# A new prologue for a spectral filter followed by a mixer: filter loads on another queue, deeper weight loading, a shorter float64 rounding and a new order

## The chip, the cores and the metric

The kernel runs on one core of one Trainium2 chip. In this kernel TensorE does the matrix products (10624 matmuls), whose results go to tiles in the memory PSUM; VectorE and ScalarE work element by element; Pool (GpSimd) and SyncE mainly issue transfers (DMA; 244 of Pool's 249 counted instructions). A "granted clock" is the profile's figure for the speed that TensorE was allowed, as a share of full speed. The metric is the device time of one execution, in microseconds (us). The kernel before took 3224.24 us (median of 3 runs, 3223.76 to 3224.53).

## The reference

The input `x` has 8 batches of 3008 positions by 256 channels. First a filter in the frequency domain, then an MLP mixer over positions and over channels. The four mixer weights are float64.

```python
X = np.fft.rfft(x, axis=1)
y = np.fft.irfft(X * (filt_r + 1j * filt_i)[None], n=3008, axis=1).astype(np.float32)
h  = np.maximum(y.transpose(0, 2, 1) @ w_tok1, 0.0) @ w_tok2      # (3008,256), (256,3008)
u  = y + h.transpose(0, 2, 1)
h2 = np.maximum(u @ w_ch1, 0.0) @ w_ch2                            # (256,1536), (1536,256)
return (u + h2).astype(np.float32)
```

## The kernel before

The transform of 3008 = 64 * 47 points is done in two steps. A batch passes through twelve length-64 transforms (a matmul, a copy by ScalarE, a store to the DRAM scratch `z`), then 32 length-47 transforms with the filter product in between (a matmul, six VectorE operations, a matmul, a copy, a store to the scratch `g`). The mixer reads `g` back into tiles called t4; its first work on a batch is a length-64 inverse transform, which VectorE copies out of PSUM as `y`.

Before the first batch can be mixed, 40 blocks of float64 weights must be rounded to float32 on the chip: 12 blocks of w1 (`w_tok1`), 16 of w2 (`w_tok2`, 376 columns each), 6 of wc1 and 6 of wc2 (512 columns each). A block lands in a staging tile as pairs of 32-bit words.

```python
    xp = pool("xp", 4)
    t4p = pool("t4p", NXC + 2)          # NXC = 12
    up = pool("up", 2)
    ...
    def filt_load():
        nc.vector.memset(filt, 0.0)
        for src, p0 in ((filt_r, 0), (filt_i, HALF)):
            nc.scalar.dma_start(filt[p0:p0 + A]..., raw(src, 0, [[64 * D, A], [1, K2 * D]]))
            lo = p0 + 32
            nc.scalar.dma_start(filt[lo:lo + A - 1, 1:K2, :],          # the mirrored rows, line 179 (L179)
                                raw(src, 63, [[64 * D, A - 1], [-D, K2 - 1], [1, D]]))
            nc.scalar.dma_start(filt[lo:lo + A, 0, :], raw(src, 32, [[64 * D, A], [1, D]]))

    def stage(n):
        return up.tile([P, n], I64, tag="u", name="st")

    def rounded(st, n, parts):          # lo, hi: the lower and upper words of the block
        ...
        nc.vector.tensor_scalar(out=top_i, in0=hi, scalar1=0x7FFFFFFF, scalar2=None, op0=ALU.bitwise_and)
        nc.vector.tensor_scalar(out=top, in0=top, scalar1=HI_MAX, scalar2=2.0 ** -112, op0=ALU.min, op1=ALU.mult)
        nc.vector.tensor_scalar(out=rest_i, in0=top_i, scalar1=3, scalar2=0x7F800000,
                                op0=ALU.logical_shift_left, op1=ALU.bitwise_and)
        nc.vector.tensor_scalar(out=top_i, in0=top_i, scalar1=3, scalar2=None, op0=ALU.logical_shift_left)
        nc.vector.scalar_tensor_tensor(out=rest, in0=lo, scalar=2.0 ** -52, in1=rest, op0=ALU.mult, op1=ALU.mult)
        nc.vector.tensor_tensor(out=top, in0=top, in1=rest, op=ALU.add)
        for src, dst in parts:          # the sign: reads hi once more
            nc.vector.scalar_tensor_tensor(out=dst.bitcast(U32), in0=src(hi), scalar=0x80000000, in1=src(top_i),
                                           op0=ALU.bitwise_and, op1=ALU.bitwise_or)
    ...
        filt_load()
        convert = weights()             # each step loads one block and rounds the one before
        for _ in dft(GROUPS[0]):        # batch 0: one block beside each step of the transforms
            next(convert, None)
        for _ in convert:
            pass
        for c in range(NXC):
            t4_load(0, c)
        ...                             # the steady phase: mixer of a batch, filter of later batches beside it
```

Of the kernel before, what the change touches and what calls it, by code (L numbers as in the profile page):

```python
# [16 lines left out]
# The sequence of 3008 = 64 * 47 positions is n = 47 * n2 + n1, with n1 = 24 * h + a.  # L17
# [7 lines left out]
K2 = 32          # residues of the frequency mod 64, up to its sign  # L25
A = 24           # n1 in two halves of 24; (h, a) = (1, 23) is padding
KR = 4 * A       # rows (h, re/im, a) of one residue
HALF = 64
HI_MAX = float(np.array(0x47EFFFFF, np.uint32).view(np.float32))    # float32's largest, as a float64's upper word
XC = 2           # columns a in one chunk of the length-64 transforms  # L30
NXC = A // XC
KC = 2           # residues in one load or store of the length-47 transforms
WC = 2           # residues in one load of their matrices
# [5 lines left out]
MT = 6           # tiles of 512 positions: four columns a, each (h, n2)  # L39
NG = 8           # n2 in one load of the second token weights  # L40
GROUPS = ((0,), (1, 2), (3, 4), (5, 6), (7,))    # batches whose filter runs together


def _make_tables():
    """The real transform of 3008 points in two steps, and its inverse.

    wa: over n2, to (h, re/im, k2) from (h, n2). The residues 0 and 32 are real and share one slot.
    wb: over n1, twiddles included, to (re/im, q), for each k2. q < 24 is the frequency k2 + 64 q, and
        q = 32 + j - 1 is 64 j - k2 (64 j - 32 for k2 = 0).
    wi, wai: the inverses of wb and wa, with the 1/N in wi; the imaginary parts of the first and  # L50
        last frequency don't count.
    """
# [3 lines left out]
    for h in range(2):  # L56
        r = slice(h * 64, h * 64 + 64)
        for k2 in range(K2):
            th = 2 * np.pi * ((n2 * k2) % N2) / N2
            c, s = np.cos(th), np.sin(th)  # L60
            re, im = h * 64 + k2, h * 64 + 32 + k2
# [47 lines left out]
def kernel(  # L109
# [20 lines left out]
    # Between the two steps the rows change partitions, by way of DRAM.  # L130
# [7 lines left out]
    xp = pool("xp", 4)  # L138
# [6 lines left out]
    t4p = pool("t4p", NXC + 2)  # L145
# [10 lines left out]

    wa = glob.tile([P, P], FP32, name="wa")
    wai = glob.tile([P, P], FP32, name="wai")
    ident = glob.tile([P, P], FP32, name="ident")
    filt = glob.tile([P, K2, D], FP32, name="filt")    # the real part on 0:64, the imaginary on 64:128  # L160
# [10 lines left out]
    def filt_load():  # L171
        nc.vector.memset(filt, 0.0)
        for src, p0 in ((filt_r, 0), (filt_i, HALF)):
            nc.scalar.dma_start(filt[p0:p0 + A].rearrange("p a d -> p (a d)"),
                                raw(src, 0, [[64 * D, A], [1, K2 * D]]))
            lo = p0 + 32
            nc.scalar.dma_start(filt[lo:lo + A - 1, 1:K2, :],
                                raw(src, 63, [[64 * D, A - 1], [-D, K2 - 1], [1, D]]))
            nc.scalar.dma_start(filt[lo:lo + A, 0, :], raw(src, 32, [[64 * D, A], [1, D]]))  # L179

    # The weights come as float64, here as 64-bit words, and are rounded to float32 on the chip.

    def stage(n):
        return up.tile([P, n], I64, tag="u", name="st")

    def rounded(st, n, parts):
        """float32 of float64: parts gives, for a view of the n elements, the views of source and destination."""
        lo, hi = (st.bitcast(U32).rearrange("p (n w) -> p n w", w=2)[:, 0:n, i] for i in range(2))
# [3 lines left out]
        # The upper word is sign, 11 bits of exponent, 20 of mantissa. Read as a float32, it times 2^-112 is  # L192
# [57 lines left out]
    def weights():  # L250
# [3 lines left out]
        for now, after in zip(steps, steps[1:] + [iter(())]):  # L254
            next(after, None)
            next(now, None)
            yield

# [1 line left out]

    xs = {}

# [256 lines left out]
```

## Time and profile before

| part of the trace | before, us |
|---|---|
| start to the first filter product (VectorE's first product operation) | 147.6 |
| start to the first copy of `y` | 339.0 |
| first copy of `y` to the end of the last matmul | 2869.8 |
| end of the last matmul to the end of the span | 13.0 |
| span of the profiled run | 3221.8 |

The reported time is some 2 us longer than the span of the same run. In the third part TensorE is busy nearly always (2851.7 of its 2869.8 us), so the question is what happens in the first 339 us. The views that tell it, the busy share by slices, stretches of the span, the chain that ended last and a piece of the timeline, are shown and read in the prediction.

### The profile page before, as it was taken

The page shows a single profiled execution, that of the slowest core. Times are in us where ns is not written, and L with a number is a line of the kernel's source. Part 1 is how long each engine was busy: PE and PEld are TensorE (multiplying, and loading weights), DVE is VectorE, ACT ScalarE, POOL GpSimd, SP SyncE. Part 2 cuts the span into 40 slices and gives each one's busy share as a digit, 9 for nine tenths or more (in the row PEclk, how much of TensorE's full clock was granted, in tenths as well). Part 3 has the DMA queues.
Part 4 walks back from the last instruction along what each step waited for, and adds up shares of the span by engine and source line. Part 5 has one row for each costly group of instructions (what it writes and reads, how often), then busy time and mean ns, then how long its engine had stood idle before and what let it go on. Part 6 is the DMA issues. An engine that isn't in the chain of part 4 may idle for free.

```text
span 3221.8 us, 26322 instructions
## 1 busy us (share of the span) xinstructions
PE 2940.4 (91%) x10624; PEld 1876.4 (58%) x10624; DVE 872.2 (27%) x1529; ACT 509.4 (16%) x889; POOL 130.3 (4%) x249
## 2 busy tenths in 40 slices
PE   0333899999999999999999999999999999999998
PEld 0111566566666566666666566666666666666665
DVE  4499105731002444301002444301023330000000
ACT  0100122211221111111221111111111111111111
POOL 1000000000000000000000000000000000000000
PEclk6555899999999999999999999999999999999999
DMA  4333232321231212110221212110221101000000
GB/s 118 123 110 110 88 111 88 100 80 48 77 86 54 60 38 62 49 56 24 77 88 54 60 38 62 47 58 23 67 62 46 41 27 42 20 13 7 7 14 13
DMA packets 130541, 189.31 MB, mean 59 GB/s; under 512 B 14498, under 2 KB 83940, under 8 KB 130372
## 3 DMA queue, kind: packets, MB, share of 16 engines
q1 hardware_dynamic: 75568, 90.93, 9.2%
q10 hardware_dynamic: 40868, 53.42, 5.6%
q0 software_dynamic: 13984, 43.27, 5.0%
q8 instruction: 85, 1.39, 0.2%
q14 instruction: 36, 0.29, 0.0%
HBM read 112.59 MB, written 74.97 MB: 58 GB/s over the span
## 4 chain that ended last, share of the span: by engine, by line
PE 89%; DVE 6%; ACTq 3%; DMA 2%; issue 0%; ACT 0%; SPq 0%; POOL 0%; POOLq 0%; DVEq 0%
PE ps_po L418 31%; PE ps_pg L398 31%; PE ps_acc L372 5%; PE ps_acc L386 5%; PE ps_b L311 3%; PE ps_i L327 3%; PE ps_a L364 3%; PE ps_po L416 3%; ACTq L179 3%; PE ps_acc L391 3%; PE ps_a L280 2%; DMA z_tmp<-t 1%; DVE top L201 1%; DVE rest L200 0%; DVE p L320 0%; DVE p L321 0%
## 5 line engine op out<-in xcount | busy, mean ns | idle before, releaser
L418 PE MATMUL ps_po<-wc,hh 128*128 128x256 f32 (+1 forms) x4608 | 1128.0, 381 | 0.0
L398 PE MATMUL ps_pg<-u,wc 128*128 128x512 f32 (+1 forms) x2304 | 1069.9, 587 | 0.0
L418 PEld LDWEIGHTS ps_po<-wc,hh 128*128 128x128 f32 (+1 forms) x4608 | 836.1, 188 | 311.2 <-issue 232.0
L401 ACT ACTIVATE hh<-ps_pg 128x512 f32<-128x512 f32 (+1 forms) x576 | 339.4, 589 | 1909.3 <-PE ps_pg L398 1830.9
L398 PEld LDWEIGHTS ps_pg<-u,wc 128*128 128x128 f32 x2304 | 430.5, 190 | 327.3 <-issue 296.4
L393 DVE COPY u<-ps_acc 128x512 f32<-128x512 f32 (+1 forms) x96 | 65.3, 681 | 781.2 <-PE ps_acc L391 781.2
L327 PE MATMUL ps_i<-p,wi 128*96 128x512 f32 (+1 forms) x320 | 153.6, 565 | 118.2 <-DVE p L322 61.4
L434 POOL DMA_DIRECT2D out_dram<-o x192 | 100.4, 529 | 2811.0 <-ACT o L430 2750.6
L317 DVE TENSOR_TENSOR p<-ps_b,filt 64x512 f32<-64x512 f32 (+1 forms) x144 | 85.4, 593 | 436.0 <-PE ps_b L311 436.0
L430 DVE COPY o<-ps_po 128x512 f32<-128x512 f32 x40 | 27.7, 692 | 612.1 <-PE ps_po L418 612.0
L386 PE MATMUL ps_acc<-w,h 128*128 128x512 f32 (+1 forms) x384 | 178.7, 588 | 11.8 <-DVE u L393 6.3
L280 PE MATMUL ps_a<-x,wa 128*128 128x512 f32 x180 | 97.2, 622 | 100.2 <-ACT t L282 89.9
L372 PE MATMUL ps_acc<-y,w 128*128 128x256 f32 x768 | 181.8, 382 | 0.0
L372 PEld LDWEIGHTS ps_acc<-y,w 128*128 128x128 f32 x768 | 147.1, 192 | 58.4 <-issue 42.7
L327 PEld LDWEIGHTS ps_i<-p,wi 128*96 128x96 f32 x320 | 54.0, 181 | 192.5 <-issue 187.3
L311 PE MATMUL ps_b<-t,wb 96*128 96x512 f32 (+1 forms) x288 | 134.9, 551 | 17.4 <-DMA t<-z_tmp 17.4
L416 PEld LDWEIGHTS ps_po<-ident,u 128*128 128x128 f32 (+1 forms) x768 | 114.3, 189 | 30.5 <-issue 23.1
L331 ACT COPY t<-ps_i 96x512 f32<-96x512 f32 (+1 forms) x160 | 79.5, 497 | 318.5 <-PE ps_i L327 318.5
L386 PEld LDWEIGHTS ps_acc<-w,h 128*128 128x128 f32 x384 | 71.6, 190 | 99.0 <-issue 80.6
L391 PEld LDWEIGHTS ps_acc<-wai,t 128*128 128x128 f32 x768 | 100.8, 192 | 44.2 <-issue 44.2
L280 PEld LDWEIGHTS ps_a<-x,wa 128*128 128x128 f32 x180 | 34.6, 197 | 145.5 <-ACT t L282 96.8
L416 PE MATMUL ps_po<-ident,u 128*128 128x128 f32 (+1 forms) x768 | 117.0, 275 | 0.0
(44 smaller groups left out, 1160.7 us busy)
## 6 DMA issues: line engine op xcount, KB each, us to landing
z_tmp<-t ACTq DMA_DIRECT2D x96, 256.0 KB
t<-z_tmp SPq DMA_DIRECT2D x128, 192.0 KB
g_tmp<-t ACTq DMA_DIRECT2D x128, 192.0 KB
t<-g_tmp SPq DMA_DIRECT2D x96, 256.0 KB
x<-in_x_dram SPq DMA_DIRECT2D x184, 128.0 KB
out_dram<-o POOLq DMA_DIRECT2D x184, 128.0 KB, 2.6
wb<-wb_t SPq DMA_DIRECT2D x80, 96.0 KB
wi<-wi_t SPq DMA_DIRECT2D x80, 96.0 KB
```

The costliest lines, as they stand in the source:

```text
L179: nc.scalar.dma_start(filt[lo:lo + A, 0, :], raw(src, 32, [[64 * D, A], [1, D]]))
L280: nc.tensor.matmul(ps, wa, xs.pop((b, c)).rearrange("p a d -> p (a d)"), start=True, stop=True)
L311: nc.tensor.matmul(ps, wbs[k // WC][:, k % WC, :], t2s[k // KC][:, k % KC], start=True, stop=True)
L327: nc.tensor.matmul(ps[0:KR], wis[k // WC][:, k % WC, :], prods.pop(k), start=True, stop=True)
L372: nc.tensor.matmul(acc[:, t, :], w1[:, a, ts(t, P)], y[:, r, :], start=(a == 0 and t == 0), stop=(a == A - 1 and t == TC - 1))
L386: nc.tensor.matmul(ps[:, 0:w], h1[:, t, ts(dh, P)], w2[:, t, ds(m * 512, w)], start=(t == 0), stop=False)
L391: nc.tensor.matmul(ps[:, ds(q * P, n)], t4[b, c][:, r, ts(dh, P)], wai[:, 0:n], start=False, stop=(q == 3))
L398: nc.tensor.matmul(ps[:, 0:w], wc1[:, c, ts(jt, P)], ut[:, c, 0:w], start=(c == 0), stop=(c == DH - 1))
L401: nc.scalar.activation(out=hh[:, 0:w], in_=ps[:, 0:w], func=AF.Relu)
L416: nc.tensor.matmul(ps[:, ts(dh, P)], ut[:, dh, ds(q * P, n)], ident, start=(q % 2 == 0 and dh == 0), stop=False)
L418: nc.tensor.matmul(ps, hh[:, ds(q * P, n)], wc2[:, jt, :], start=False, stop=(end and q in (1, 2)))
L434: nc.gpsimd.dma_start(rows[:, lo:lo + n, :], o[h * HALF:(h + 1) * HALF, 0:n, :])
```

## The change

The intent is to shorten the prologue. The filter loads leave ScalarE's queue for the Pool queue and are split so that 16 and 7 partitions are loaded apart; five weight loads are to be in flight; the rounding gives its first operation to ScalarE and keeps five on VectorE; w1 is rounded beside the length-64 transforms, and everything else after the products. The staging tiles move into the pool of the t4 tiles, which now has seven buffers, and a t4 tile holds four columns instead of two. The diff, cut to its core:

```diff
-    t4p = pool("t4p", NXC + 2)
+    t4p = pool("t4p", A // TC4 + 1)                  # 24 // 4 + 1 = 7
     def filt_load():
-        nc.vector.memset(filt, 0.0)
         for src, p0 in ((filt_r, 0), (filt_i, HALF)):
-            nc.scalar.dma_start(filt[p0:p0 + A]...
+            nc.gpsimd.dma_start(filt[p0:p0 + A]...
-            nc.scalar.dma_start(filt[lo:lo + A - 1, 1:K2, :],
-                                raw(src, 63, [[64 * D, A - 1], [-D, K2 - 1], [1, D]]))
+            for j0, n in ((0, 16), (16, A - 1 - 16)):
+                nc.gpsimd.dma_start(filt[lo + j0:lo + j0 + n, 1:K2, :],
+                                    raw(src, 63 + 64 * j0, [[64 * D, n], [-D, K2 - 1], [1, D]]))
...
     def stage(n):
-        return up.tile([P, n], I64, tag="u", name="st")
+        return t4p.tile([P, n], I64, tag="t4", name="st")
     def rounded(st, n, parts):
+        nc.scalar.activation(out=top, in_=hi_f, func=AF.Copy, scale=2.0 ** -112)
         nc.vector.tensor_scalar(out=top_i, in0=top_i, scalar1=3, scalar2=None, op0=ALU.logical_shift_left)
+        nc.vector.scalar_tensor_tensor(out=top_i, in0=hi, scalar=0x80000000, in1=top_i,
+                                       op0=ALU.bitwise_and, op1=ALU.bitwise_or)
+        nc.vector.tensor_scalar(out=rest_i, in0=top_i, scalar1=0xFF800000, scalar2=None, op0=ALU.bitwise_and)
         nc.vector.scalar_tensor_tensor(out=rest, in0=lo, scalar=2.0 ** -52, in1=rest, op0=ALU.mult, op1=ALU.mult)
         for src, dst in parts:
-            nc.vector.scalar_tensor_tensor(out=dst.bitcast(U32), ...)
+            nc.vector.tensor_tensor(out=dst, in0=src(top), in1=src(rest), op=ALU.add)
...
     def weights():
+        for s in steps[0:AHEAD]:                     # AHEAD = 5: loads of the first five blocks
+            next(s)
+        yield
+        for i, s in enumerate(steps):
+            next(s, None)                            # round block i, then load block i + 5
+            if i + AHEAD < len(steps):
+                next(steps[i + AHEAD])
             yield
...
+        next(convert)
         filt_load()
-        for _ in dft(GROUPS[0]):
-            next(convert, None)
+        for i, _ in enumerate(dft(GROUPS[0])):
+            if i < A // 2:
+                next(convert)
+        for c in range(A // TC4):
+            t4_load(0, c)
         for _ in convert:
             pass
-        for c in range(NXC):
-            t4_load(0, c)
```

Cut are the other order of rows of `z` and `g` (their transfers have one outer dimension where they had two), `xp` with three buffers instead of four, the new tile for the last piece of `x`, the order of the wc1 blocks and of a few small loads, and the clamp at float32's largest value (HI_MAX) with the masking of the sign, which the new rounding leaves out.

More of the change, by code (lines that the diff above doesn't have):

```diff
@@ L28 @@
 HALF = 64
-HI_MAX = float(np.array(0x47EFFFFF, np.uint32).view(np.float32))
 XC = 2
 NXC = A // XC
+TC4 = 4
 KC = 2
@@ L40 @@
 NG = 8
+AHEAD = 5
 GROUPS = ((0,), (1, 2), (3, 4), (5, 6), (7,))
@@ L60, in _make_tables @@
             c, s = np.cos(th), np.sin(th)
-            re, im = h * 64 + k2, h * 64 + 32 + k2
+            re, im = 4 * k2 + 2 * h, 4 * k2 + 2 * h + 1
             wa[r, re] = c
@@ L137 @@
     glob = pool("glob", 1)
-    xp = pool("xp", 4)
+    xp = pool("xp", 3)
     t1p = pool("t1p", 3)
@@ L155, in bank @@
         return (psg if tag == "pg" else psum).tile([P, 512], FP32, tag=tag, name="ps_" + tag)
+    xlast = glob.tile([P, XC, D], FP32, name="xlast")
     wa = glob.tile([P, P], FP32, name="wa")
@@ L171, in filt_load @@
     def filt_load():
-        nc.vector.memset(filt, 0.0)
         for src, p0 in ((filt_r, 0), (filt_i, HALF)):
-            nc.scalar.dma_start(filt[p0:p0 + A].rearrange("p a d -> p (a d)"),
+            nc.gpsimd.dma_start(filt[p0:p0 + A].rearrange("p a d -> p (a d)"),
                                 raw(src, 0, [[64 * D, A], [1, K2 * D]]))
             lo = p0 + 32
-            nc.scalar.dma_start(filt[lo:lo + A - 1, 1:K2, :],
-                                raw(src, 63, [[64 * D, A - 1], [-D, K2 - 1], [1, D]]))
-            nc.scalar.dma_start(filt[lo:lo + A, 0, :], raw(src, 32, [[64 * D, A], [1, D]]))
+            for j0, n in ((0, 16), (16, A - 1 - 16)):
+                nc.gpsimd.dma_start(filt[lo + j0:lo + j0 + n, 1:K2, :],
+                                    raw(src, 63 + 64 * j0, [[64 * D, n], [-D, K2 - 1], [1, D]]))
+            nc.gpsimd.dma_start(filt[lo:lo + A, 0, :], raw(src, 32, [[64 * D, A], [1, D]]))
     def stage(n):
-        return up.tile([P, n], I64, tag="u", name="st")
+        return t4p.tile([P, n], I64, tag="t4", name="st")
     def rounded(st, n, parts):
-        lo, hi = (st.bitcast(U32).rearrange("p (n w) -> p n w", w=2)[:, 0:n, i] for i in range(2))
+        words = [st.bitcast(t).rearrange("p (n w) -> p n w", w=2)[:, 0:n] for t in (U32, FP32)]
+        lo, hi, hi_f = words[0][:, :, 0], words[0][:, :, 1], words[1][:, :, 1]
         top = hp.tile([P, 512], FP32, tag="hh", name="top")[:, 0:n]
@@ L191, in rounded @@
         top_i, rest_i = top.bitcast(U32), rest.bitcast(U32)
-        nc.vector.tensor_scalar(out=top_i, in0=hi, scalar1=0x7FFFFFFF, scalar2=None, op0=ALU.bitwise_and)
-        nc.vector.tensor_scalar(out=top, in0=top, scalar1=HI_MAX, scalar2=2.0 ** -112, op0=ALU.min, op1=ALU.mult)
-        nc.vector.tensor_scalar(out=rest_i, in0=top_i, scalar1=3, scalar2=0x7F800000,
-                                op0=ALU.logical_shift_left, op1=ALU.bitwise_and)
+        nc.scalar.activation(out=top, in_=hi_f, func=AF.Copy, scale=2.0 ** -112)
         nc.vector.tensor_scalar(out=top_i, in0=top_i, scalar1=3, scalar2=None, op0=ALU.logical_shift_left)
+        nc.vector.scalar_tensor_tensor(out=top_i, in0=hi, scalar=0x80000000, in1=top_i,
+                                       op0=ALU.bitwise_and, op1=ALU.bitwise_or)
+        nc.vector.tensor_scalar(out=rest_i, in0=top_i, scalar1=0xFF800000, scalar2=None, op0=ALU.bitwise_and)
         nc.vector.scalar_tensor_tensor(out=rest, in0=lo, scalar=2.0 ** -52, in1=rest, op0=ALU.mult, op1=ALU.mult)
-        nc.vector.tensor_tensor(out=top, in0=top, in1=rest, op=ALU.add)
         for src, dst in parts:
-            nc.vector.scalar_tensor_tensor(out=dst.bitcast(U32), in0=src(hi), scalar=0x80000000, in1=src(top_i),
-                                           op0=ALU.bitwise_and, op1=ALU.bitwise_or)
+            nc.vector.tensor_tensor(out=dst, in0=src(top), in1=src(rest), op=ALU.add)
     def w1_load(i):
@@ L250, in weights @@
     def weights():
-        steps = [f(i) for f, n in ((w1_load, A // 2), (w2_load, TC * N2 // NG), (wc1_load, DH * DC // 512),
-                                   (wc2_load, JT // 2)) for i in range(n)]
-        next(steps[0])
-        for now, after in zip(steps, steps[1:] + [iter(())]):
-            next(after, None)
-            next(now, None)
+        steps = ([w1_load(i) for i in range(A // 2)] + [w2_load(i) for i in range(TC * N2 // NG)]
+                 + [wc1_load(c * (DC // 512) + q) for q in range(DC // 512) for c in range(DH)]
+                 + [wc2_load(i) for i in range(JT // 2)])
+        for s in steps[0:AHEAD]:
[5 more added lines that the diff above has]
+                next(steps[i + AHEAD])
             yield
@@ L263, in x_load @@
     def x_load(b, c):
-        t = xp.tile([P, XC, D], FP32, tag="x", name="x")
+        last = c == NXC - 1
+        t = xlast if last else xp.tile([P, XC, D], FP32, tag="x", name="x")
         rows = x[b].rearrange("(n2 n1) d -> n2 n1 d", n1=N1)
-        last = c == NXC - 1
-        if last:
-            nc.vector.memset(t[HALF:P, XC - 1, :], 0.0)
         for h in range(2):
@@ L273, in x_load, with rows_of @@
         xs[b, c] = t
-    def rows_of(t_d, b, c):
-        return t_d[b].rearrange("k (g a) d -> g k a d", a=A)[:, :, ts(c, XC), :]
+    def rows_of(t_d, b):
+        return t_d[b].rearrange("k (g a) d -> (k g) a d", a=A)
     def a_unit(b, c, tag):
@@ L282, in a_unit @@
         nc.scalar.copy(out=t1.rearrange("p a d -> p (a d)"), in_=ps)
-        nc.scalar.dma_start(rows_of(z_d, b, c), t1)
+        nc.scalar.dma_start(rows_of(z_d, b)[:, ts(c, XC), :], t1)
     def dft(bs):
@@ L291, in dft @@
         for i, u in enumerate(todo):
+            a_unit(*u, ("a", "b")[i % 2] if first else "a")
             if i + 3 < len(todo):
                 x_load(*todo[i + 3])
-            a_unit(*u, ("a", "b")[i % 2] if first else "a")
             yield
@@ L354, in t4_load @@
     def t4_load(b, c):
-        t4[b, c] = t4p.tile([P, XC, D], FP32, tag="t4", name="t4")
-        nc.sync.dma_start(t4[b, c], rows_of(g_d, b, c))
+        t4[b, c] = t4p.tile([P, TC4, D], FP32, tag="t4", name="t4")
+        nc.sync.dma_start(t4[b, c], rows_of(g_d, b)[:, ts(c, TC4), :])
     def token_hidden(b):
@@ L363, in token_hidden @@
                 ps = bank("a")
-                nc.tensor.matmul(ps, wai, t4[b, c].rearrange("p a d -> p (a d)"), start=True, stop=True)
+                nc.tensor.matmul(ps, wai, t4[b, c * XC // TC4][:, ds(c * XC % TC4, XC), :].rearrange("p a d -> p (a d)"),
+                                 start=True, stop=True)
                 ys[c] = yp.tile([P, XC, D], FP32, tag="y", name="y")
@@ L388, in u_unit @@
         for q in range(4):
-            c, r = divmod(4 * m + q, XC)
+            c, r = divmod(4 * m + q, TC4)
             n = min(P, w - q * P)
@@ L445, in u_part @@
             if dh == DH - 1 and b + 1 < B:
-                wait.extend((2 * m, 2 * m + 1))
+                wait.append(m)
         for dh in range(DH):
@@ L466 @@
     with tc.manual_schedule():
-        for t, src in ((wa, wa_d), (wai, wai_d), (ident, id_d)):
-            nc.sync.dma_start(t, src)
-        filt_load()
-        convert = weights()
-        for _ in dft(GROUPS[0]):
-            next(convert, None)
+        nc.sync.dma_start(wa, wa_d)
+        nc.vector.memset(xlast[HALF:P, XC - 1, :], 0.0)
+        nc.vector.memset(filt, 0.0)
+        convert = weights()
+        next(convert)
+        filt_load()
+        for i, _ in enumerate(dft(GROUPS[0])):
+            if i == 0:
+                for t, src in ((wai, wai_d), (ident, id_d)):
+                    nc.scalar.dma_start(t, src)
+            if i < A // 2:
+                next(convert)
+        for c in range(A // TC4):
+            t4_load(0, c)
         for _ in convert:
             pass
-        for c in range(NXC):
-            t4_load(0, c)
         for bs, after in zip(GROUPS, GROUPS[1:] + ((),)):
```

## The prediction

> **What bounds the kernel now.** I read the page first, to find where TensorE is not full. These are the 40 slices of 80.5 us each, busy tenths, then the granted clock:
>
> ```profile
> PE   0333899999999999999999999999999999999998
> DVE  4499105731002444301002444301023330000000
> PEclk6555899999999999999999999999999999999999
> ```
>
> TensorE is full from the fifth slice on, starved in the first four. Next, stretches of the span (columns: length; busy us and count of PE, PEld, DVE, ACT, POOL; granted clock; DMA share; GB/s):
>
> ```profile
> 40.00:80.00 40.00, 0.00 (x0) 0.00 (x0) 12.03 (x23) 0.00 (x0) 4.29 (x8) 0.50 0.35 88
> 160.00:200.00 40.00, 12.31 (x25) 6.79 (x26) 37.87 (x99) 2.21 (x6) 3.77 (x7) 0.50 0.41 119
> ...
> 440.00:800.00 360.00, 357.62 (x1261) 220.22 (x1260) 151.55 (x222) 68.61 (x117) 12.61 (x24) 1.00 0.28 83
> ```
>
> From 440 us TensorE is 99% busy at full clock and nothing in that phase can be shortened by other engines. Before that there are two limits: at 40 to 80 us nothing computes, and at 160 to 200 us VectorE is 95% busy. The chain that ended last names them (start, us, what):
>
> ```profile
> 12.18 50.15 ACTq L179
> 63.10 34.97 ACTq L179
> ...
> 159.09 0.97 DVE w L203 x3
> ...
> 336.90 2.09 PE ps_a L364 x2
> 339.01 0.70 DVE y L366
> ```
>
> So the prologue is: until 98 us ScalarE's queue is held by the two mirrored filter loads of L179, behind which wait its copies out of PSUM; to 146 us the 12 length-64 transforms and their stores; to 327 us VectorE, sharing itself between the filter products and the rounding of 28 of 40 weight blocks; then the first y copy at 339.0 us, after which TensorE runs to the end. The total after is therefore 3224.2 minus however much earlier that y copy comes. In what follows I call its time Y.
>
> [...] L179 has 23 rows[...]: 713 KB in 34.97 us is 20.9 GB/s, and from 80 to 98 us the DMA share stands at 0.07, one sixteenth, at 24 GB/s. [...] The trace has no such copy out of SBUF; its copy out of PSUM took 587 ns.
>
> **The change, part by part.** The steady phase keeps its matmuls and their order, so it keeps its length. Only Y moves. The built program has three stages before it.
>
> Stage A, to the first filter product. Removed: the 85 us (50.15 + 34.97) in which ScalarE's queue stood still. Its 12 copies and stores now interleave with the first operation of 12 w1 roundings, and the filter goes out on the Pool queue behind five w1 loads. What must move before the first product: w1 6.0 MB, x 3.1, z 3.1, filter 3.0, tables and about two w2 blocks 0.9, 16 MB in all. The rate comes from the only stretch with all of x, w1 and filter in flight:
>
> ```profile
> 4.00:6.00 2.00, 0.00 (x0) 0.00 (x0) 2.00 (x1) 0.00 (x0) 0.00 (x0) 1.00 1.07 239
> 6.00:8.00 2.00, 0.00 (x0) 0.00 (x0) 2.00 (x1) 0.00 (x0) 0.00 (x0) 1.00 1.03 237
> 8.00:10.00 2.00, 0.00 (x0) 0.00 (x0) 1.93 (x3) 0.00 (x0) 0.00 (x0) 1.00 1.04 237
> ```
>
> 16 MB at 237 GB/s is 68 us, from 2 us on, plus some 5 us for the last z store, its load back and one matmul: stage A ends at about 75 us instead of 146. Full use of the DMA engines all the way is optimistic; fewer w2 bytes ahead would help. I take 75, from 64 to 88.
>
> Stage B, the 32 filter products alone on VectorE. Before, they shared it with weights:
>
> ```profile
> 150.31 0.36 DVE L194 TENSOR_SCALAR top<-st 128x376 uint32<-128x376 uint32 x1
> ...
> 153.80 0.41 DVE L317 TENSOR_TENSOR p<-ps_pg,filt 64x256 f32<-64x256 f32 x1
> ...
> 156.48 0.36 DVE L194 TENSOR_SCALAR top<-st 128x376 uint32<-128x376 uint32 x1
> 156.60 1.14 PE L327 MATMUL ps_i<-p,wi 128*96 128x256 f32 x2 [4.24 <-DVE p L322]
> ...
> 157.53 1.06 PE L311 MATMUL ps_pg<-t,wb 96*128 96x256 f32 x2
> ```
>
> One product takes 156.48 - 153.80 = 2.68 us of VectorE; the two matmuls behind it, even at half clock, end 2.1 us after it (158.59 against 156.48), so VectorE sets the pace: 32 x 2.68 = 86 us. Stage B ends at 161.
>
> Stage C, the 28 remaining blocks (16 of w2, 12 of wc1 and wc2), which now stand on VectorE after all products and ahead of the y copies. First the arithmetic. A w2 block took 3.49 us (150.31 to 153.80), a block of 512 took 3.78 (9.44 to 13.22). The new form moves the scaling by 2^-112 to ScalarE, drops the masking of the sign ahead of it and puts the sign back early with one scalar_tensor_tensor (0.58 with its gap, 0.72 for 512, as those of before); five operations are left, together 2.8 us for w2 and 3.0 for 512. If VectorE set the pace, stage C would be 16 x 2.8 + 12 x 3.0 = 81 us and Y about 245.
>
> But it does not, and this is the step that decides. The stages now share seven buffers with the t4 tiles, and the program issues the six t4 loads of batch 0 before the remaining weights. Five blocks of w2 are already loaded; six of the seven buffers then stay with t4 until the mixer has used them. In the built program the 23 later blocks all have one address, and each load waits for the previous block's fourth VectorE operation (the lower word's product, the last reader of the stage). "Five in flight" is one in flight, with nothing beside it. The landing times come from the loads of before, from issue to landing, w2 and then wc1:
>
> ```profile
> DMA to landing us min/median/max: 3.2/3.4/5.6
> ...
> DMA to landing us min/median/max: 3.7/3.8/4.0
> ```
>
> One turn for w2: Pool notices 0.35 (VectorE ended about 153.8, the issue started 154.18), landing 3.3, wake-up 0.15 (a w1 load issued at 45.75 took 3.9 and VectorE started at 49.84),[...] hand-over 0.07, four operations 1.9: 6.27 us. For 512: 0.35 + 3.8 + 0.15[...] + 0.07 + 2.3 = 7.28. Stage C: 2.6 us for the last inverse matmul, copy, store and the first ScalarE operation; the five loaded blocks to the fourth operation of the last, 4 x 2.8 + 1.9 = 13; 11 x 6.27 = 69; 12 x 7.28 = 87; the last addition 0.7; some 3 for the t4 loads, 3.1 MB, in the way at the start. Sum 175. With stage A and B, Y = 75 + 86 + 175 = 336 against 339. The 71 us won in stage A and the 1.0 us shaved off each block are paid back as load latency. The main phase starts 3 us earlier: 3221. Landing with an otherwise idle DMA may be shorter than the times above, which lay beside other traffic; 0.2 us on 23 loads is 5 us, so I settle a little lower, at 3217.
>
> **The rivals.** First, stage C runs at VectorE's pace, Y = 245, time 3130, 2.9% faster. It is what the change intends, and the 81 us are sound; against it stands the chain of waits in the built program, which leaves no second buffer. I give it little. Second, stage A is longer: in the old trace the DMA fell to 171 GB/s at 12 to 14 us and to 24 to 28 when loads waited for buffers; if the new order averages 170, stage A lasts 16 MB / 170 = 94 us plus 7, Y = 362, time 3247, 0.7% slower. For it speaks[...] that w1 block 5 queues behind all of the filter. Third,[...] t4 loads of twice the size and xp of three buffers change the steady phase. Waits there are 18 us of TensorE in total, all on VectorE and ScalarE, none on a DMA; I see no more than 5 us either way.
>
> **Range and chances.** Stage A can be 11 us shorter or 13 longer; stage C, 23 turns, with 0.4 us of doubt in each, 9 us either way; stage B and the main phase 3. Combined as independent, some 16 us down and 18 up, so 3199 to 3236. A 2% gain needs 3160, Y = 275: stage C would have to be 60 us shorter, 2.6 us off each turn. A 2% loss needs Y = 403. Chances 0.04, 0.93, 0.03.
>
> **What would show it right or wrong.** ScalarE starts its first copy near 10 us, not 99. The first product comes at 64 to 88 us; products follow each other at 2.68 us. In stage C, VectorE is less than half busy, POOL's loads are 6.3 and then 7.3 us apart, each preceded by a wait for the L204 operation, and ScalarE's first operation waits for the DMA 23 times. The first y copy is at 320 to 355 us and from there to the end it is 2885 us, as before. Wrong would be loads closer than 5 us or overlapping, a first product after 95 us, or TensorE waiting for DMA in the main phase.

The trace of before shows: the second load of L179 at 20.9 GB/s with a DMA share of 0.07, a tensor_tensor of 512 on VectorE in 692 ns, and a copy of 512 out of PSUM on ScalarE in 587 ns. From each turn of stage C the term for ScalarE's operation is cut. The sums came to 6.27 and 7.28 us with it, and they are what the further working uses; the terms that are left add up to 5.77 and 6.67. The 2.6 us ahead of the five loaded blocks hold the same operation once. The total of 175 us for stage C, Y = 336 and the time of 3217 us stand.

## The result and the profile after

The changed kernel took 3231.24 us (median of 4 runs, 3230.55 to 3233.05), the kernel before 3224.26 us in the same rounds. A ratio here is the mean time of one kernel's fast runs over that of the other's of the same rounds, so it is not quite the ratio of the quoted medians. It is 1.0021, with a 95% interval of 1.0007 to 1.0035: the same within 2%, and slower by 0.2%.

| part of the trace | before | predicted | after |
|---|---|---|---|
| stage A: to the first filter product | 147.6 | 75 | 85.9 |
| stage B: to the last inverse matmul of the products | mixed with weights | 86 | 85.9 |
| stage C: from there to the first `y` copy | mixed with products | 175 | 180.0 |
| first `y` copy | 339.0 | 336 | 351.8 |
| from there to the end of the last matmul | 2869.8 | | 2869.4 |
| end of the last matmul to the end of the span | 13.0 | | 7.5 |

The page's busy tenths, in 40 slices of 80.7 us:

```profile
PE   3610699999999999999999999999999999999999
DVE  4954204751001434401001434401023330001000
PEclk9999999999999999999999999999999999999999
```

TensorE now has work in the first two slices, little in the third and nothing in the fourth; the fifth stands at 6 tenths, where it was 8 before, and from the sixth on both rows are full. VectorE falls to 4 and 2 tenths in the fourth and fifth. The clock row is full from the start, which it was not before, but that differs from run to run: two of the four runs show a mean clock of 0.955 and two of 0.999, and both pairs took between 3230.5 and 3233.1 us.

Stretches of the span (length; busy us and count of PE, PEld, DVE, ACT, POOL; granted clock; DMA share; GB/s):

```profile
20.00:30.00 10.00, 1.30 (x2) 0.50 (x2) 0.19 (x1) 0.89 (x2) 1.11 (x2) 1.00 0.97 113
30.00:40.00 10.00, 2.79 (x3) 0.50 (x2) 5.58 (x10) 2.06 (x4) 0.59 (x2) 1.00 1.13 173
40.00:50.00 10.00, 2.05 (x2) 0.50 (x2) 2.93 (x6) 0.00 (x0) 1.55 (x3) 1.00 0.91 153
...
240.00:280.00 40.00, 0.00 (x0) 0.00 (x0) 16.76 (x38) 2.93 (x5) 3.20 (x6) 1.00 0.23 66
440.00:800.00 360.00, 357.61 (x1250) 219.27 (x1249) 151.38 (x221) 69.06 (x118) 12.58 (x24) 1.00 0.27 84
```

The first three are in stage A. The DMA engines count as busy nearly all the time and yet move only 113 to 173 GB/s, where I had counted with 237. The fourth is in stage C: nothing on TensorE, VectorE busy for 42%, the DMA for 23%; nothing is at its limit, so they are waiting for each other. The last is the steady phase, as before.

The chain that ended last, cut to the turn of stage and load where w2 goes over to wc1 (start, us, what; the view lists only the longer pieces, so two of the four VectorE operations up to L204, the last reader, are missing; the fifth comes after the next load is released):

```profile
84.68 1.21 PE ps_b L316 x2
171.77 1.15 PE ps_i L332 x2
...
261.90 3.89 DMA st<-in_moe_w_ch_dram
265.87 0.67 ACT top L198
267.03 0.70 DVE top L200
268.21 0.70 DVE rest L204
268.95 0.51 issue
269.46 3.90 DMA st<-in_moe_w_ch_dram
...
351.78 0.61 DVE y L372
```

This is the loop that replaced the old limits. A load lands (3.89 us), ScalarE scales the block, VectorE rounds it up to L204, which is the last reader of the staging tile, and only then, 0.55 us after L204's end at 268.91, does the next load start. From one load's start to the next, 7.56 us pass. The waits of the same stretch say it once more (who waited, for whom: us in total, times, longest):

```profile
POOL st L241 <- DVE rest L204: 40.6, 6, 7.0
ACT top L198 <- DMA st<-in_moe_w_ch_dram: 81.4, 12, 7.2
```

Pool holds each of the six wc1 loads back for VectorE's L204, and ScalarE waits for the DMA in all twelve blocks of wc1 and wc2.

ScalarE's new operation, by shape (busy us, mean ns, idle before and what ended it):

```profile
L198 ACT ACTIVATE top<-st 128x512 f32<-128x512 f32 x24 | 15.9, 663 | 118.5 <-DMA st<-in_moe_w_ch_dram 81.4 <-DMA filt<-in_filt_r_dram 20.8 <-DMA x<-in_x_dram 9.3
L198 ACT ACTIVATE top<-st 128x376 f32<-128x376 f32 x16 | 8.5, 538 | 77.6 <-DMA st<-in_moe_w_tok_dram 70.2 <-DVE w L206 7.0 <-ACT t L336 0.4
```

It takes 663 and 538 ns, reading every second word of a float32 view in SBUF; from the two lengths, that is 0.92 ns an element and 193 ns fixed. The terms that the prediction counted for it were smaller. In the first row 20.8 us of the waits in stage A ended with a filter transfer.

Last, the end of the span, which the prediction did not look at. The timeline of before (start, us, engine, line, operation, count, idle before):

```profile
3202.41 6.37 PE L418 MATMUL ps_po<-wc,hh 128*128 128x256 f32 x24
...
3209.85 1.05 POOL L434 DMA_DIRECT2D out_dram<-o  x2 [0.32 <-DVE o L428]
```

and of after:

```profile
3214.82 6.37 PE L424 MATMUL ps_po<-wc,hh 128*128 128x256 f32 x24
...
3224.27 1.56 POOL L440 DMA_DIRECT2D out_dram<-o  x3 [2.85 <-issue]
```

The last matmuls end at 3208.78 and 3221.19. Before, the stores were issued at once and the span then went on to 3221.8; after, Pool paused 2.85 us and the span ended at 3228.7. So 13.0 us followed the last matmul before, and 7.5 after. Neither profile shows what fills this time, and in e10 the span ended 5.2 us after the last matmul although Pool did not pause there, so the pause alone does not explain them. The spread goes through all the runs whose ends were read: 13.0 us before and in e4 and e6, 5.2 in e10, and 7.5 to 8.0 in the changed kernel, e1, e2, e3, e5, e9, e11 and e12. What decides it stays open. The 5.5 us have to be taken out when stages are compared through the total: the `y` copy is 12.8 us later, the total only 7.0.

### The profile page after: what moved, and what is told of

It is laid out like the page before. It is cut to its first block, busy times and chain, and to the rows that moved or that the text cites. A ratio compares the mean times of both kernels' runs of the same rounds, so it can differ in the third digit from the quotient of the medians.

```text
span 3228.7 us, 26261 instructions
## 1 busy us (share of the span) xinstructions
PE 2941.8 (91%) x10624; PEld 1876.0 (58%) x10624; DVE 843.9 (26%) x1442; ACT 532.0 (16%) x929; POOL 134.7 (4%) x257
## 4 chain that ended last, share of the span: by engine, by line
PE 88%; DMA 5%; DVE 5%; issue 1%; ACT 1%; SPq 0%; POOL 0%; ACTq 0%; POOLq 0%
PE ps_po L424 31%; PE ps_pg L404 30%; PE ps_acc L378 5%; PE ps_acc L392 5%; PE ps_b L316 3%; PE ps_i L332 3%; PE ps_po L422 3%; PE ps_acc L397 3%; PE ps_a L369 3%; PE ps_a L285 2%; DMA x<-in_x_dram 2%; DMA st<-in_moe_w_ch_dram 1%; DMA st<-in_moe_w_tok_dram 1%; DVE rest L204 1%; DVE top L200 1%
## 5 line engine op out<-in xcount | busy, mean ns | idle before, releaser
L369 PE MATMUL ps_a<-t,wai 128*128 128x512 f32 x192 | 100.9, 607 | 182.9 <-DVE y L372 175.9
L322 DVE TENSOR_TENSOR p<-ps_b,filt 64x512 f32<-64x512 f32 (+1 forms) x144 | 85.5, 594 | 437.2 <-PE ps_b L316 436.7
L369 PEld LDWEIGHTS ps_a<-t,wai 128*128 128x128 f32 x192 | 36.3, 193 | 195.6 <-DVE y L372 183.3
## 6 DMA issues: line engine op xcount, KB each, us to landing
out_dram<-o POOLq DMA_DIRECT2D x184, 128.0 KB, 2.5
x<-in_x_dram SPq DMA_DIRECT2D x176, 128.0 KB, 3.3
```

The lines of the kernel that those rows point to most:

```text
L322: nc.vector.tensor_tensor(out=p1[re], in0=ps[re], in1=fr, op=ALU.mult)
L369: nc.tensor.matmul(ps, wai, t4[b, c * XC // TC4][:, ds(c * XC % TC4, XC), :].rearrange("p a d -> p (a d)"), start=True, stop=True)
```

## Experiments

The theory: stage C is one load in flight, because six of the seven buffers are held by t4 tiles that nobody frees before stage C ends; the rival is that stage C has another limit (VectorE, or the weights' transfer itself). For stage A, the theory is that the filter's own transfers are slow. The first four kernels ran on one chip in the same rounds, three rounds each, beside the kernel before (3224.37 us).

**e1: the six t4 loads issued after the weights.** The same instructions in another order, so that all seven buffers rotate among the staging tiles.

```diff
-        for c in range(A // TC4):
-            t4_load(0, c)
         for _ in convert:
             pass
+        for c in range(A // TC4):
+            t4_load(0, c)
```

> The changed kernel with one move: the six t4 loads of batch 0 come after the last weight block instead of before the 23 late ones. My theory: the t4 tiles held six of the seven stage buffers, so that the late loads ran one at a time at 6.5 us (w2) and 7.4 us (512) a turn; with the buffers free VectorE sets the pace at 2.8 and 3.0 us. Then stage C falls from 180 us to 2.6 + 13 + 11 x 2.8 + 12 x 3.0 + 1 = 83 us, the first y copy comes at about 255 us instead of 351.8 and the time is about 3134 us (3128 to 3148). Rival: the loads are slow by themselves, one in flight or five: no change, 3231 us.

Measured: 3134.82 us, ratio 0.9724 (0.9708 to 0.9740), correct. First product 86.8 us, first `y` copy 255.9. Pool's loads in the timeline of stage C:

```profile
188.88 0.54 POOL L227 DMA_DIRECT2D st<-in_moe_w_tok_dram  x1 [2.26 <-DVE rest L204]
191.68 0.54 POOL L227 DMA_DIRECT2D st<-in_moe_w_tok_dram  x1 [2.26 <-DVE rest L204]
```

They are 2.80 us apart, which is the time of five VectorE operations (0.36, 0.55, 0.36, 0.55 and 0.93 us, and their gaps), and not 6.5. Pool still waits for an L204 each time, but for that of an earlier block. With stage B at 86 us, stage C took 255.9 - 86.8 - 86 = 83 us; the rounding alone had been worked out to 81. The theory holds, the rivals fall: the place of one loop is worth 96 us. (Stage A is untouched here and in e2, and took 86.8 and 87.9 us against 85.9: a difference of 2 us in stage A says nothing.)

**e2: two staging buffers instead of one.** The order of the change is kept; the blocks that would get the single free buffer go to the pool `up`, whose two buffers are idle there.

```diff
+    made = []
+
     def stage(n):
+        made.append(n)
+        if len(made) > A // 2 + AHEAD:
+            return up.tile([P, n], I64, tag="u", name="st")
         return t4p.tile([P, n], I64, tag="t4", name="st")
```

> The changed kernel in its order, but the 23 late blocks get their stage from the pool of u, which has two buffers and is not used yet. If the latency of a single load in flight is what stage C is made of, two in flight halve it, down to VectorE's pace at the least: 6.5/2 = 3.25 and 7.4/2 = 3.7 us a block, stage C 2.6 + 13 + 11 x 3.25 + 12 x 3.7 + 1 = 97 us instead of 180, time about 3148 us (3140 to 3165). If anything other than the number of buffers holds the loads back (the Pool queue, its semaphores): 3231 us or little less.

Measured: 3149.30 us, ratio 0.9768 (0.9753 to 0.9782), first `y` copy 270.9. In the timeline of Pool, where wc1 (L246) goes over to wc2 (L252):

```profile
236.81 0.53 POOL L246 DMA_DIRECT2D st<-in_moe_w_ch_dram  x1 [3.57 <-DMA st<-in_moe_w_ch_dram]
...
244.41 0.73 POOL L252 DMA_DIRECT2D st<-in_moe_w_ch_dram  x1 [3.74 <-DMA st<-in_moe_w_ch_dram]
```

Two loads start every 7.6 us, so 3.8 a block: the same turn as before, shared by two. The view names a DMA as releaser, since one landed last before the issue; but each issue comes 0.55 us after the last reader of its buffer ended (236.26 to 236.81, 243.85 to 244.41), as in the changed kernel. The number of free buffers sets stage C, step by step: one gives 7.5 us for a block of 512, two 3.8, seven VectorE's pace (2.98 in e1).

**e3: the kernel before with the new filter loads alone** (the Pool queue, 16 and 7 rows).

```diff
     def filt_load():
         nc.vector.memset(filt, 0.0)
         for src, p0 in ((filt_r, 0), (filt_i, HALF)):
-            nc.scalar.dma_start(...)        # three per part, the mirrored one of 23 rows
+            nc.gpsimd.dma_start(...)        # four per part, the mirrored ones of 16 and 7 rows
```

> The kernel before with one part of the change alone: the filter loads on the Pool queue, the mirrored rows split into 16 and 7. ScalarE's queue is then free from the start. Theory: stage A is not simply 85 us shorter, because the 14 weight blocks that stand ahead of the first product now wait behind the filter on the Pool queue, with two buffers, at about 6.2 us each (12.4 us a pair in the trace of before): first product at 30 + 14 x 6.2 = 117 us instead of 146, then 193 us to the first y copy as before, so y at 310 and a time of about 3195 us (3175 to 3210). Rival: all 85 us come through: 3140 us.

Measured: 3194.90 us, ratio 0.9909 (0.9894 to 0.9924). The total is as expected, but two errors cancel in it. The first product came at 125.6 us, 9 later than expected, and the `y` copy at 317.2, 7 later; and from that copy to the end of the span it was 2877.2 us, 5.6 less than in the kernel before, because the end came soon after the last matmul, as in the changed kernel. What the filter loads give in the old order is read from the trace: the `y` copy 21.8 us earlier. One new wait stands in stage A: the w1 blocks now queue behind the filter on Pool's queue, and VectorE waited 50.5 us for one of them.

**e4: the kernel before with the new rounding alone.**

```diff
-    def rounded(st, n, parts):      # seven VectorE operations
+    def rounded(st, n, parts):      # one of ScalarE, five of VectorE
```

> The kernel before with another part alone: the new rounding, one ScalarE operation and five on VectorE. Each of the 28 shared turns (6.15 and 6.45 us) becomes 0.7 us shorter, 20 us. But the first 12 blocks now need ScalarE, whose queue stands still until 98 us with the filter loads, so they move from 10 to 62 us to after 98 us: first product at about 98 + 14 x 5.5 = 175 us instead of 146. Sum: about 9 us slower, 3233 us (3215 to 3250). Rival: the saving on VectorE comes through, 3204 us.

Measured: 3209.34 us, ratio 0.9953 (0.9939 to 0.9968): outside the expected 3215 to 3250. Two parts lie in it. From the first product to the `y` copy it took 172.7 us instead of 191.4, so the shorter rounding saved 18.7 us where VectorE was the limit (95% busy from 160 to 200 us, in both kernels); 20 was expected. But stage A, which I expected to lose 29 us because ScalarE now stood between the w1 loads and VectorE, lost 4 (first product at 151.5 us). ScalarE's queue in the timeline:

```profile
12.28 31.86 ACTq L179 DMA_DIRECT2D filt<-in_filt_r_dram  x1
44.91 34.32 ACTq L179 DMA_DIRECT2D filt<-in_filt_i_dram  x1
```

The first mirrored load held the queue for 31.86 us, not 50.15: with the w1 roundings stuck behind ScalarE, Pool issued no w1 loads between 3.5 and 85.5 us. The queue was free at 79.2 us instead of 98.1, and w1 then came quickly. My expectation had taken the 98 us as given. (The 31.86 us alone show the shorter time; that the missing w1 loads are its cause is inferred.)

The next four kernels ran on another chip, beside 3224.70 us for the kernel before.

**e5: the change with the old rounding.** The seven VectorE operations of before in the new prologue.

```diff
-    def rounded(st, n, parts):      # one of ScalarE, five of VectorE
+    def rounded(st, n, parts):      # seven VectorE operations
```

> The changed kernel with the old rounding (seven VectorE operations, none on ScalarE; the last one still reads the stage). In stage C the turn is latency plus all operations up to the last reader of the stage: w2 0.55 + 3.45 + 0.2 + 3.5 = 7.7 us instead of 6.5, blocks of 512 0.55 + 3.8 + 0.2 + 3.8 = 8.35 instead of 7.4; 11 x 1.2 + 12 x 0.95 = 25 us more, and 5 x 0.7 = 3 for the loaded blocks: 3259 us (3245 to 3270). If the loads alone set the pace and VectorE's work were hidden: 3231 to 3236 us.

Measured: 3244.74 us, ratio 1.0061 (1.0044 to 1.0078), first `y` copy 367.2. Loads in stage C:

```profile
303.27 0.53 POOL L243 DMA_DIRECT2D st<-in_moe_w_ch_dram  x1 [7.37 <-DVE wc L207]
311.42 0.53 POOL L243 DMA_DIRECT2D st<-in_moe_w_ch_dram  x1 [7.62 <-DVE wc L207]
```

This turn takes 8.15 us; the eleven turns of 512 average 8.02, 0.56 more than in the changed kernel, and ten of w2 7.27, 0.73 more than its 6.54. The rival, that rounding is hidden behind the loads, is excluded: with one buffer it adds to the turn. The size was expected too large (8.35 and 7.7 a turn): Pool noticed the end of the old form in 0.28 us, where 0.55 was counted, and VectorE started 0.03 us after a landing, where 0.2 was counted.

**e6: the change without the filter loads** (wrong on purpose, one look).

```diff
         next(convert)
-        filt_load()
         for i, _ in enumerate(dft(GROUPS[0])):
```

> Wrong result on purpose: the changed kernel without its eight filter loads (the filter stays zero). It measures what they cost stage A, whose first product came at 85.9 us instead of 75: from 20 to 50 us the DMA moved 113 to 173 GB/s although its engines were busy. If the filter loads slow down everything beside them, the stretch goes with them: 13 MB at 237 GB/s and 7 us, first product at about 62 us. If they cost only their bytes at the usual rate, 3 MB at 237 GB/s = 13 us: about 73 us.

Measured: the first product at 56.3 us instead of 85.9, earlier still than the theory had it. Stretches of the span:

```profile
20.00:30.00 10.00, 5.84 (x6) 1.18 (x5) 8.25 (x15) 4.11 (x7) 2.37 (x4) 1.00 1.05 303
30.00:40.00 10.00, 6.13 (x6) 1.50 (x6) 8.75 (x16) 3.81 (x8) 3.27 (x6) 1.00 1.05 307
```

The same 10 us that moved 113 and 173 GB/s now move 303 and 307, with the DMA engines as busy. The filter's 3 MB of the 16 MB cost 29.6 us; the other 13 MB took 56.3 us less the 2 at the start and the 5 at the end, that is about 264 GB/s. So stage A is long because of the filter's transfers, and everything else is quicker than I had counted. The 29.6 us can hold two things: the transfers themselves, and the w1 loads behind them on Pool's queue, of which the changed kernel's trace shows six held back until a filter transfer had landed, 31.3 us in all. Why the filter's transfers are slow was asked with four kernels, each with one look; the number is the first product's time, 85.9 us in the changed kernel.

**e7: the mirrored rows read in rising order** (wrong).

```diff
-                                    raw(src, 63 + 64 * j0, [[64 * D, n], [-D, K2 - 1], [1, D]]))
+                                    raw(src, 33 + 64 * j0, [[64 * D, n], [D, K2 - 1], [1, D]]))
```

> Wrong result on purpose: the mirrored filter rows are read upwards, 31 KB in a piece, instead of downwards in steps of 1 KB; same bytes,[...] same rows 64 KB apart. If the pieces of 1 KB in falling order are what slows the stretch from 20 to 50 us, the first product comes at about 75 us; if not, at 86 us.

Measured: first product at 90.9 us. Falling addresses in pieces of 1 KB are not the cause; the edit took effect, since the result is wrong (relative error 0.90).

**e8: a pitch of 62 rows instead of 64 between partitions** (wrong), 62 KB instead of 64 KB in DRAM.

```diff
-    raw(src, 0, [[64 * D, A], [1, K2 * D]])        raw(src, 63 + 64 * j0, [[64 * D, n], ...])
+    raw(src, 0, [[62 * D, A], [1, K2 * D]])        raw(src, 63 + 62 * j0, [[62 * D, n], ...])
```

> Wrong result on purpose: the large filter loads read rows 62 KB apart instead of 64 KB; pieces, order[...] as in the changed kernel. If the power of two between rows that are read side by side is what slows the stretch from 20 to 50 us, the first product comes at about 75 us; if not, at 86 us.

Measured: first product at 87.3 us. The power of two is not the cause.

The next two ran on a third chip (kernel before: 3224.49 us).

**e9: real and imaginary part in turn.** In the changed kernel all loads of the real part (partitions 0 to 23 and 32 to 55) go out ahead of those of the imaginary part. Issued in turn, loads of both parts are in flight together. The first range is for an order that matters, the second for one that does not.

```diff
-        for src, p0 in ((filt_r, 0), (filt_i, HALF)):
-            (four loads)
+        for each of the four loads:
+            for src, p0 in ((filt_r, 0), (filt_i, HALF)):
+                (that load)
```

> The changed kernel with its eight filter loads in another order: real and imaginary part by turns instead of all of the real part first. Without filter loads the first product came at 56 us instead of 86, so 3 MB of filter cost 30 us. [...] the cost falls by about half: first product at 68 to 76 us. [...] the order changes little: 83 to 88 us.

Measured: 3228.68 us, correct; first product at 85.1 us. A stretch of the span:

```profile
30.00:40.00 10.00, 0.54 (x1) 0.00 (x0) 2.55 (x5) 0.04 (x1) 1.09 (x2) 1.00 0.90 116
```

The slow stretch stays as slow (116 GB/s here, 113 at the lowest in the changed kernel). The order of the two parts isn't the cause.

**e10: 24 rows as 16 and 8.** This asks whether the split of the 24-row loads is the cause. The first range is for a split that matters, the second for one that does not.

```diff
-            nc.gpsimd.dma_start(filt[p0:p0 + A]..., raw(src, 0, [[64 * D, A], [1, K2 * D]]))
+            for j0, n in ((0, 16), (16, A - 16)):
+                nc.gpsimd.dma_start(filt[p0 + j0:p0 + j0 + n]..., raw(src, 64 * j0, [[64 * D, n], [1, K2 * D]]))
```

> The changed kernel with the two direct filter loads of 24 rows split into 16 and 8 rows[...]; order, bytes and partitions as they were. [...] first product at 70 to 80 us;[...] at 84 to 90 us[...].

Measured: 3231.34 us, correct; first product at 91.3 us. The split of the 24-row loads isn't the cause; the loads of 7 rows were left as they were.

A rival that none of these four touches is the queue itself. The single packets of the packed trace bear on it: the real part's 24-row load went out in 24 packets of 32 KB in both kernels. On ScalarE's queue before, they took 5.2 us in all (11.41 to 16.65, 150 GB/s); on Pool's queue after, 10.2 us (16.95 to 27.14). Other traffic differed too, so this is a hint and not a test; filter loads on a third queue, or on ScalarE's in the new split, were not run.

The last two are versions that should beat both kernels, on the same chip, three rounds each (kernel before: 3224.66 us).

**e12: e1, and w2 rounded before the products.** While x, w1 and the filter are coming, VectorE is half idle (in the changed kernel busy for 42.0 of the first 86 us); the w2 blocks, loaded through seven buffers, go ahead of the products.

```diff
             if i < A // 2:
                 next(convert)
+            elif i < A // 2 + 2:
+                for _ in range(TC * N2 // NG // 2):     # eight blocks of w2 at each of two steps
+                    next(convert)
```

> The control to it: t4 loads last and w2 before the first product, but all filter loads in a row behind the first five w1 loads, as in the changed kernel. The w1 blocks then end at about 83 us as there, 16 x 2.8 = 45 us of w2 follow, first product at about 128 us, 86 + 3 + 37 after it: y at about 254 us, time 3133 us (3124 to 3140), as in the first experiment: moving blocks from behind the products to before them gains nothing while VectorE still waits through the filter. If it is much faster than that, the order of the blocks alone did it and not the spread.

Measured: 3132.71 us (3130.57 to 3133.49), ratio 0.9716 (0.9699 to 0.9732), correct. First product 128.0 us, first `y` copy 252.3. It is the fastest median, but not to be told apart from e1 (0.9708 to 0.9740, on another chip).

**e11: e12, with one filter load issued beside each w1 block**, instead of all eight in a row.

```diff
         for src, p0 in ((filt_r, 0), (filt_i, HALF)):
             nc.gpsimd.dma_start(...)
+            yield                       # and so after each load
...
             if i < A // 2:
                 next(convert)
+                next(filters, None)
```

> A version meant to beat both: t4 loads last as in the first experiment, the 16 blocks of w2 rounded before the first product, and the eight filter loads given out one by one between the weight loads. In the first experiment VectorE had 213 us of work before the first y copy (7 for memsets, 40 blocks of 2.8 or 3.0, 86 for products) and y came at 256: 43 us of waiting, nearly all in stage A. If the filter's 30 us of slow DMA can lie beside rounding, stage A ends when its 19 MB (70 us at 275 GB/s) and the filter's 30 us are through, first product at about 100 us, then 86 + 3 + 12 x 3.0 + 1: y at about 226 us, time about 3106 us (3095 to 3122). If every block behind a filter load waits as long as it did, y stays near 255: 3130 to 3138 us.

Measured: 3134.40 us, ratio 0.9720 (0.9706 to 0.9735), first product 130.3 us: the 27 us that I hoped for against e12 (3106 against 3133) did not come. (The 275 GB/s in the expectation is the estimate after e6, which gave about 264 for the bytes counted in its stage A; its trace shows 285 over the first 50 us.) Two stretches, late in its stage A:

```profile
60.00:70.00 10.00, 4.09 (x4) 1.00 (x4) 6.39 (x12) 3.08 (x5) 1.59 (x3) 1.00 0.99 167
70.00:80.00 10.00, 2.04 (x2) 0.50 (x2) 4.16 (x8) 1.24 (x2) 1.07 (x2) 1.00 0.99 180
```

The DMA engines are full here as well, at 167 and 180 GB/s. The slow stretch was spread over 20 to 80 us (168 to 232 GB/s in the slices before these), not shortened: spreading the filter's transfers did not make them cheaper.

## Why the prediction was right

The prediction said "the same", with 3217 us; it was 3231, inside the range of 3199 to 3236. The sign differs: 0.2% slower instead of 0.2% faster. The total was helped by luck: stages A and C together came 15.8 us later than predicted, and 5.5 us at the end of the span, which it did not look at, gave some of that back. Three slips in its working changed nothing: the fifth slice of TensorE is at 8 tenths and not full; "1.0 us shaved off each block" is 0.7 to 0.8 by its own figures; its doubts combine to some 15 us down and 16 up, so the printed range is a little wider than its working. By its own steps:

- **The step that decides, one load in flight, was right.** e1 gives the other buffers back and stage C falls from 180 to 83 us; e2 gives one more and halves the turn. The first rival (stage C at VectorE's pace, 3130) is nearly what e1 measured, 3134.8: its arithmetic was good, and only the buffers spoke against it.
- **The signs named beforehand** were there: ScalarE's first copy starts at 9.95 us, VectorE is 42% busy in stage C, the late loads start 6.54 and 7.46 us apart (named: 6.3 and 7.3), the chain holds 23 of them, 11 of w2 and 12 of wc1 and wc2, and the `y` copy is between 320 and 355 us. One sign failed: from that copy to the end it was not 2885 us but 5.5 less than before, as the last point says.
- **Stage B was right**: 85.9 against 86. In e12's trace the granted clock stands at half in this stage (0.50 from 130 to 215 us, against 1.00 in the changed kernel), and it took 85.8 us there too (128.0 to 213.8), so TensorE's speed indeed does not set it.
- **Stage A was 11 us too short** (75 against 85.9). The term that failed is "16 MB at 237 GB/s". The rate was taken at 4 to 10 us of the old trace, as a stretch "with all of x, w1 and filter in flight"; but in the timeline of that trace the first filter load of all is issued at 10.40 us, after the memset of the filter's tile, and the chain starts the first mirrored one at 12.18: that stretch held nothing of the filter. e6 shows what stood in its place: 13 MB at about 264 GB/s and 29.6 us for the filter's 3 MB. The second rival, an average of 170 GB/s, was nearer in mechanism (a low rate while the filter loads, and w1 loads held behind it, for 31.3 us in all) but too pessimistic in size. Why the filter's transfers are slow remains open after e7, e8, e9 and e10. VectorE's work beside them is not it: from 20 to 30 us, at 113 GB/s, VectorE was busy for 0.19 us.
- **Stage C was 5 us too short** (175 against 180.0). From the last inverse matmul to the first late load it took 16.2 us where 19 with the t4 loads were counted. Eleven turns of w2 took 74.0 us instead of 69: the first 8.6, since its load landed only after 5.45 us, in step with the t4 loads expected to be "in the way at the start", and ten of 6.54 instead of 6.27. The rest, wc1 and wc2 to the `y` copy, took 89.9 instead of some 88. Two terms of the turn were too small: Pool's notice, 0.55 us instead of 0.35, and ScalarE's operation, which took 0.663 and 0.538. The landing was within 0.1 us of the estimate; the 4 us that I took off for a landing "shorter than the times above" were wrong, with 3.29 to 3.48 us for the late w2 loads.
- **The main phase was right to 0.4 us up to the last matmul, and 5.5 us shorter behind it.** The third rival allowed 5 us either way, for other reasons; the stores and buffers that it named changed nothing (the three waits of TensorE for VectorE's copies and ScalarE's activations were 6.3, 6.3 and 5.5 us and are 5.5, 6.3 and 5.5, none for a DMA). So the sum is 336 + 2885 + 15.8 (stages A and C) - 5.5 (the end of the span) = 3231.

The rest of the gain that the change intended is answered by the experiments: in the old order, the filter loads alone are worth 22 us at the `y` copy (e3), the rounding 15 us (e4), and in the new order the rounding again gives 15 us at the `y` copy (367.2 in e5 against 351.8). In the changed kernel the 62 us won in stage A, and what the rounding saves, went into 23 loads that waited for each other. One edit, e1, makes the change what it was meant to be, 2.8% faster than before.

## What to carry to other kernels

The depth of a prefetch is the number of buffers that are free at that point of the program, not the number of loads that the code issues ahead: count who holds each buffer, and when it is given back (here one buffer gave 7.5 us a block of 512, two 3.8, seven 2.98). Take a transfer rate only from a stretch of the trace in which the very transfers that you count are in flight (237 GB/s was counted, 113 to 173 were found), and take the end of the span out before you read a stage from a total (13.0 us before, 7.5 after).
